# Another list of due dates, and other landing times, for a planner that writes a kernel's order

## The chip, the cores and the metric

The kernel runs on one core of a Trainium2 chip. A core has TensorE (PE), VectorE (DVE), ScalarE (ACT), GpSimd (POOL) and SyncE (SP), each with a queue of its own. The metric is the time of one execution on the device in microseconds.

## What is computed

Block-sparse attention is followed by a residual token-and-channel MLP, both for 4 batches of 768 tokens. Attention has 8 heads of 64; the MLP sees them as 512 channels, with 2048 hidden ones.

```python
mask = |block_i - block_j| <= 1, first and last block, 3 sampled blocks a row   # blocks of 32
attn = softmax(where(mask, q @ k.T / 8, -1e9)) @ v          # [4, 8, 768, 64]
x    = attn.transpose(0, 2, 1, 3).reshape(4, 768, 512)
u    = x + lam * einsum('ts,bsd->btd', w_tok, alpha1 * x + beta1)
out  = u + lam * (relu((alpha2 * u + beta2) @ w_ch1) @ w_ch2)
```

## The kernel before

**Tiling.** Two heads of one batch make a pair; there are 16 pairs (`NP`), four a batch. A pair's scores (two heads of 768 x 768, in 128-row tiles) are cut into 9 units of 1024 columns, so there are 144 units. For each unit PE makes QK into two PSUM banks (`sps`), ACT makes exp into an `eT` tile (L966, one of 7), and PE multiplies `eT` with `vext` (PV, L990) into a `gb` bank. In the first six pairs (`T0`) the mask rides in 24 additional rows of q and k (L928), and q and k come through PE transposes (L426), evacuated by DVE or ACT. In the later ten, three units are one batch (L947): two 64-row matmuls lie beside each other in the array, q and k come by transposing DMAs on SP's queue, and DVE multiplies the mask in (L971).

After a pair, DVE normalizes (L1006, L1009) into `x_sb` and makes `a1p` (L1162, L1173) with alpha1 and beta1 already multiplied by lam (`a1l`, `b1l`, L652 and L659); PE multiplies with the transposed w_tok (token matmuls, L1211); DVE adds them to `x_sb` (L1235) and makes `ub` (L1249), which is transposed into `uT`. After a batch's four pairs follow the channel products, in two halves of 384 tokens (`kk` from 0 to 7): 16 first products (`ch1`, L1358), each with a relu on DVE or ACT (L1405, L1397), and 3 x 4 groups of four second products (`ch2`, L1438), each 512 columns; the last group row of the last half is split into 384 and 128 columns. DVE adds the result to `x_sb` (L1460) and SP stores it (L1479).

**The order.** After a part written by hand (to L464), everything is an `Op` in a list `pl.ops` of 1408, with the engines that may run it, their prices in ns, a due date, and what it depends on. `Plan.run` (L170) plays time forward: whenever an engine is free, it starts that ready operation with the lowest due date for which buffers are there, and emits its instructions then. `pin_order` (L55) keeps each engine's order. So due dates and prices set only the order of each queue; on the chip semaphores decide the times. POOL issues all loads after the start (`load`, L539), SP the transposing DMAs and the stores.

Dates (`due0`) run from -46 to 208, one unit of date for each unit of attention. Then 67 seeds each move some dates near one place by random steps (L1493 to L1499):

```python
for op in pl.ops:
    if abs(op.due0 - mid) < wide and r.random() < part:
        op.due += r.gauss(0, step)
```

**What the planner takes for the first loads.** The load queue begins at `self.dma` = 6900; a load lands 700 ns after its share of the queue (L496 to L501). v of pair 0 lands at 7500 (L599), the second heads of the first q and k at 7000 and 6800 (`("f", i)`, L898), be2T at 6500 (L667). DVE is free from 6300, PE from 5950, ACT from 6100 (L469). On DVE wait at the start: three row copies (`row`, L905), two casts of the second heads (`fc`, L421), be2T's copy (`be2c`, L666) and the copies of v (`putv`, L1028). Matmuls on a constant (`fill`, L394) have dates from 1000: PE takes one only when nothing else is ready.

Of the kernel before, what the change touches and what calls it, by code (L numbers as in the profile page):

```python
# [44 lines left out]
EXPB = -0.35667494  # L45
T0 = 6
FINE = 3
SEEDS = [3340310007, 3340310011, 3340310015, 3340310024, 3340310026, 3340310027, 3340310065, 3340310070, 3340310081, 3340310120, 3340310138, 3340310152, 3340310166, 3340310177, 3340310178, 3340310179, 3340310340, 3340310371, 3340310405, 3340310518, 3340310537, 3340310574, 3340310590, 3340310686, 3340310729, 1340310788, 1340310806, 1340310822, 1340310954, 1340310957, 3340311162, 3340311192, 3340311406, 3340311549, 3340312202, 3340312526, 3340312534, 1340312821, 1340312995, 2340313211, 2340313318, 1340313338, 3340313793, 1340314038, 1340314057, 1340314590, 1340315664, 3340316245, 1363480032, 1363480039, 3363480372, 3363480518, 1363480765, 4363481891, 4363482185, 4363482912, 4363483188, 1382590026, 4382590413, 4382590423, 4382590431, 2382580781, 1382591202, 2382582015, 2382583582, 4382594112, 1382594473]
NFILL = 24
ORD = ((0, 2, 4, 1, 3, 5), (1, 3, 5, 0, 2, 4))  # L50
HF = 3 * S
# [51 lines left out]
class Plan:  # L103
# [3 lines left out]
    def __init__(self, pools, free):  # L107
        self.pools = {k: list(range(n)) for k, n in pools.items()}
        self.free = dict(free)
        self.ops = []  # L110
        self.users = {}
        self.slot = {}
        self.held = {}
        self.reader = {}
        self.shifted = False
        self.exps = 0
        self.dma = 6900.0
        self.ring = []
        self.occ = None
        self.loads = []  # L120
        self.hw = 0.0
        self.segs = []
# [47 lines left out]
    def run(self):  # L170
# [13 lines left out]
        while count:  # L184
            for r in [r for r in release if r[0] <= t]:
                release.remove(r)
                self.pools[r[1]].append(r[2])
            moved = True
            while moved:
                moved = False  # L190
                best = {}
                idle = [e for e in self.free if self.free[e] <= t]
                held = [(o.due, o.n) for o in cand if o.hold and o.ready <= t and len(self.pools["sps"]) == 2]
                held = min(held) if held else None
                for op in cand:
                    if op.ready > t:
                        continue
                    if held and op.need and (op.due, op.n) > held:
                        if any(n[1][0][0] in ("gb", "sps") for n in op.need):
                            continue  # L200
                    opts = [o for o in op.opts if o[0] in idle]
                    r = self.reader.get(op.reads)
                    if r and r[1] > t:
                        opts = [o for o in opts if o[0] == r[0]]
                    opts = [
                        o
                        for o in opts
                        if o[0] not in best
                        or (op.due, op.n) < (best[o[0]][0].due, best[o[0]][0].n)
                    ]  # L210
                    if not opts:
                        continue
                    taken = {}
                    for need in op.need:
                        p = self.place(need, taken)
                        if p is None:
                            break
                        taken[p] = taken.get(p, 0) + 1
                    else:
                        for o in opts:  # L220
                            best[o[0]] = (op, o)
                if not best:
                    break
                for op in cand:
                    if op.urgent and op.ready > t:
                        for o in op.opts:
                            if o[0] in best and best[o[0]][0].due > op.due:
                                if op.ready - t < best[o[0]][1][1]:
                                    del best[o[0]]
                if best:  # L230
                    op, (e, occ, vis) = min(best.values(), key=lambda x: (x[0].due, x[0].n))
                    for need in op.need:
                        p = self.place(need, {})
                        self.slot[need[0]] = (p, self.pools[p].pop(0))
                    op.start = t
                    op.eng = e
                    self.now, self.shifted = op, False
                    if callable(vis):
                        vis = vis(self, t)
                    if self.shifted:  # L240
                        for x in cand:
                            x.ready = max([d.vis for d in x.deps] + [0])
                    op.vis = t + vis
                    if op.reads:
                        self.reader[op.reads] = (e, op.vis)
                    self.free[e] = t + (self.occ or occ)
                    self.occ = None
                    for k in op.uses:
                        self.users[k] -= 1
                        self.held[k] = max(self.held.get(k, 0), op.vis)  # L250
                        if not self.users[k]:
                            release.append((self.held[k],) + self.slot[k])
                    if op.name[0] == "exp":
                        self.exps += 1
                    cand.remove(op)
                    count -= 1
                    for h in heirs.get(id(op), []):
                        h.left -= 1
                        if not h.left:
                            h.ready = max([d.vis for d in h.deps] + [0])  # L260
                            cand.append(h)
                    op.emit(op)
                    moved = True
            later = [x for x in self.free.values() if x > t]
            later += [r[0] for r in release if r[0] > t]
            later += [op.ready for op in cand if op.ready > t]
            if count and not later:
                raise RuntimeError(f"stuck: {[o.name for o in cand[:20]]}")
            if count:
                t = min(later)  # L270
# [3 lines left out]
def kernel(  # L274
# [54 lines left out]
    wtk = wk.tile([P, NT, S], BF, name="wtk", tag="w2b", bufs=1)  # L329
# [209 lines left out]
    def load(name, cost, due, emit, packet=70, **kw):  # L539
        return pl.add(name, [("POOL", 720, queued(cost, packet))], due, emit, **kw)  # L540
# [8 lines left out]
    def load_pair(pi, what="qkv"):  # L549
        b, n = divmod(pi, NPAIR)  # L550
        for w in what:
            key = (w, pi)
            src = dict(q=q, k=k, v=v)[w]

            def emit(op, key=key, src=src, w=w):
                nc.gpsimd.dma_start(ld[w][sl(key)][:], pair_ap(src, b, n))  # L556

            LD[key] = load(
                ("load",) + key,
                1020,  # L560
                9 * pi - (6 if w == "v" else 12 if pi < T0 else 20),
                emit,
                need=[(key, [(w, 0)])],
            )
# [6 lines left out]
    def bc_load(nm, t, src, due):  # L571
        def emit(op):
            nc.gpsimd.dma_start(t[:], src.unsqueeze(0).to_broadcast([P, DM]))

        BC[nm] = load(("bc", nm), 1640 if nm == "lam" else 640, due, emit)

    def emit_wtk(g):
        return lambda op: nc.gpsimd.dma_start(
# [17 lines left out]

        return f

    LD[("v", 0)] = landed(("v", 0), 7500)  # L599
    pl.slot[("v", 0)] = ("v", 0)  # L600
    pl.pools["v"].remove(0)
    for g in range(3):
        WT.append(load(("wtk", g), 2500, (-4, 1, 2)[g], emit_wtk(g)))
    bc_load("lam", lam_bc, moe_lam, 8)
    bc_load("a1", a1_bc, moe_alpha1, 8.1)
    bc_load("b1", b1_bc, moe_beta1, 8.2)
# [285 lines left out]
    for i in range(2):  # L892
        op = pl.dve(
            ("fc", i),
            dve(384, 2),
            1 + 0.1 * i,
            lambda op, i=i: first_cast(1, i, nc.vector.tensor_copy),
            deps=[landed(("f", i), 7000 - 200 * i)],  # L898
        )
        FC1.append(op)  # L900
    ROWS = []
# [143 lines left out]
    i = 0  # L1045
# [444 lines left out]
                    uses=[okey],  # L1490
                )

    for seed in SEEDS:  # L1493
        r = random.Random(seed)
        part, step = r.choice([0.02, 0.1, 0.3, 1]), r.choice([0.3, 1, 3])
        mid, wide = r.uniform(0, 300), r.choice([4, 12, 40])
        for op in pl.ops:
            if abs(op.due0 - mid) < wide and r.random() < part:
                op.due += r.gauss(0, step)  # L1499
    pl.run()  # L1500
    pin_order(nc, tc)

# [29 lines left out]
```

## Time and profile before

| | us |
|---|---|
| median of three runs | 306.15 (305.70 to 306.36) |
| the profiled execution | 305.65 |
| its span, first to last instruction | 303.9 |
| first planned matmul starts | 5.84 |
| the final stretch of `ch2` matmuls starts | 290.45 |
| DVE's last addition starts | 301.05 |
| TensorE's granted clock | 1.000 |

The span is what the profile shows; the time has another 1.75 us around it. A timeline line gives the start, the length, the engine, the line of the kernel, the operation, the tiles it writes and reads, their shapes, how many instructions are merged, and in brackets the engine's idle time before it with what ended it. Ends of matmuls are modelled, starts are not. Of the 368 matmuls of 512 columns at L1438, 339 are in the trace; the records of the others are missing.

The first loads by the trace, issue and landing in us:

| load | issued | landed | load | issued | landed |
|---|---|---|---|---|---|
| q, second head | 2.44 | 7.30 | k1 | 5.02 | 12.55 |
| k, second head | 1.78 | 5.81 | wtk1 | 5.72 | 14.40 |
| be2T | 2.19 | 7.06 | wtk2 | 6.26 | 16.27 |
| v0 | 3.07 | 8.72 | v1 | 6.79 | 17.67 |
| wtk0 | 3.76 | 10.60 | k2 | 7.49 | 18.56 |
| q1 | 4.33 | 11.60 | beta1 | 9.01 | 19.24 |
| alpha1 | 11.88 | 21.25 | lam | 12.84 | 21.89 |

### The profile page before, as it was taken

The numbers are of one execution on the slowest core, as the hardware profiler recorded it, in microseconds if no ns is written. First come the engines' busy times: TensorE is split into PE (matmuls) and PEld (weight loads), VectorE is DVE, ScalarE is ACT, GpSimd is POOL, SyncE is SP. The second block draws the span as 40 slices with busy tenths as digits, with TensorE's granted clock in tenths as the row PEclk, the third lists the DMA queues.
The fourth block names the chain that finished last, engine by engine and source line by source line (L and its number), as shares of the span: only waits on it lengthen the run. The fifth ranks groups of instructions, "written<-read, shape, count | busy, mean of one in ns | idle before, by whom it ended". The sixth has DMA issues, their size and how long they took to land.

```text
span 303.9 us, 7142 instructions
## 1 busy us (share of the span) xinstructions
PE 297.7 (98%) x2962; PEld 186.3 (61%) x2991; DVE 234.7 (77%) x443; ACT 175.8 (58%) x240; POOL 45.2 (15%) x71
## 2 busy tenths in 40 slices
PE   7999999999999999999999999999999999999997
PEld 3777878765665575556755665555665564555544
DVE  7679998999799699858977896878778763856532
ACT  4998799898587665778576454766567520000000
POOL 9467252413010102010000000000000000000000
PEclk9999999999999999999999999999999999999999
DMA  7999999999877717745262225024030005000011
GB/s 149 202 256 204 206 204 206 198 160 150 159 118 126 117 52 133 137 90 111 45 109 50 66 63 105 36 63 86 2 86 37 0 2 156 3 35 35 37 66 72
DMA packets 50672, 31.38 MB, mean 103 GB/s; under 512 B 27784, under 2 KB 47056, under 8 KB 50640
## 3 DMA queue, kind: packets, MB, share of 16 engines
q0 software_dynamic: 17520, 15.47, 33.7%
q1 hardware_dynamic: 32796, 15.06, 21.6%
q8 instruction: 23, 0.38, 0.5%
q10 hardware_dynamic: 324, 0.39, 0.4%
q14 instruction: 9, 0.07, 0.1%
HBM read 30.78 MB, written 6.29 MB: 122 GB/s over the span
## 4 chain that ended last, share of the span: by engine, by line
PE 88%; ACT 7%; DMA 2%; issue 1%; POOL 1%; DVE 0%; ACTq 0%; POOLq 0%
PE gb L1358 27%; PE gb L1438 27%; PE gb L1211 10%; PE gb L990 10%; ACT eT L966 7%; PE sps L947 4%; PE sps L928 4%; PE gb L947 3%; DMA v<-in_v_dram 2%; PE gb L426 1%; PE sps L1211 0%; POOL wtokT L378 0%; POOL be2T L386 0%; PE gb L394 0%; PE sps L1358 0%
## 5 line engine op out<-in xcount | busy, mean ns | idle before, releaser
L966 ACT ACTIVATE eT<-sps 128x1024 f16<-128x1024 f32 x114 | 110.9, 1033 | 6.8 <-PE sps L928 5.4
L1358 PE MATMUL gb<-uT,w1b 128*128 128x384 bf16 (+1 forms) x508 | 92.4, 326 | 0.0
L1438 PE MATMUL gb<-w2b,hts 128*128 128x512 bf16 (+2 forms) x371 | 88.4, 370 | 1.6 <-issue 0.2
L1358 PEld LDWEIGHTS <-w1b 128*128 128x128 bf16 x512 | 48.0, 98 | 32.7 <-issue 1.2
L971 DVE TENSOR_TENSOR eT<-eT,msk 128x1024 f16<-128x1024 f16 x90 | 58.8, 684 | 9.7 <-ACT eT L966 9.7
L1438 PEld LDWEIGHTS <-hts 128*128 128x128 bf16 x400 | 35.9, 97 | 36.9 <-issue 3.2
L990 PEld LDWEIGHTS <-eT 128*128 128x128 f16 x1152 | 47.9, 97 | 14.8 <-issue 3.8
L1405 DVE TENSOR_SCALAR hts<-gb,b1t 128x384 bf16<-128x384 f32 x72 | 44.3, 616 | 15.7 <-PE gb L1358 14.1
L966 ACT ACTIVATE eT<-gb 128x512 f16<-128x512 f32 x60 | 32.5, 594 | 40.2 <-PE gb L947 40.1
L990 PE MATMUL gb<-vext,eT 128*128 128x65 f16 x1152 | 53.2, 193 | 0.2 <-DVE vext L1028 0.2
L1397 ACT ACTIVATE hts<-gb,b1t 128x384 bf16<-128x384 f32 x55 | 31.8, 585 | 16.5 <-PE gb L1358 14.1
L1211 PE MATMUL gb<-a1p,wtokT 128*128 128x256 bf16 (+1 forms) x348 | 34.0, 250 | 0.0
L1211 PEld LDWEIGHTS <-wtokT 128*128 128x128 bf16 x360 | 29.2, 98 | 6.1 <-issue 1.6
L928 PE MATMUL sps<-qk 88*128 88x512 bf16 (+1 forms) x144 | 31.6, 325 | 0.4
L1460 DVE TENSOR_TENSOR ot<-x_sb,gb 128x512 f32<-128x512 f32 (+2 forms) x25 | 16.6, 663 | 16.2 <-PE gb L1438 15.9
L1235 DVE TENSOR_TENSOR x_sb<-x_sb,gb 128x512 f32<-128x512 f32 (+1 forms) x25 | 15.8, 641 | 5.2 <-PE gb L1211 5.0
L1009 DVE TENSOR_TENSOR x_sb<-gb,rcp 128x384 f32<-128x384 f32 x32 | 17.8, 557 | 1.1
L947 PE MATMUL sps<-qk 64*128 64x256 bf16 x180 | 17.9, 305 | 0.0
L947 PEld LDWEIGHTS <-qk 64*128 64x128 bf16 x240 | 9.3, 94 | 12.5 <-issue 8.2
L1249 DVE TENSOR_TENSOR ub<-x_sb,a_bc 128x512 bf16<-128x512 f32 (+1 forms) x26 | 16.2, 645 | 0.4
L556 POOL DMA_DIRECT2D q<-in_q_dram x15 | 10.8, 720 | 36.4 <-DMA qk<-q 28.8
L1162 DVE TENSOR_TENSOR a1p<-x_sb,a_bc 128x768 bf16<-128x768 f32 (+1 forms) x17 | 15.4, 905 | 0.2
(74 smaller groups left out, 165.0 us busy)
## 6 DMA issues: line engine op xcount, KB each, us to landing
out_dram<-ot SPq DMA_DIRECT2D x23, 256.0 KB, 2.0
v<-in_v_dram POOLq DMA_DIRECT2D x16, 192.0 KB, 6.8
q<-in_q_dram POOLq DMA_DIRECT2D x15, 192.0 KB, 6.6
k<-in_k_dram POOLq DMA_DIRECT2D x15, 192.0 KB, 7.0
w1b<-in_moe_w_ch_dram POOLq DMA_DIRECT2D x4, 512.0 KB, 12.1
w2b<-in_moe_w_ch_dram POOLq DMA_DIRECT2D x4, 512.0 KB, 13.2
qk<-qk SPq DMA_DIRECT2D x20, 96.0 KB, 3.5
wtk<-in_moe_w_tok_dram POOLq DMA_DIRECT2D x3, 384.0 KB, 8.7
```

The costliest lines, as they stand in the source:

```text
L928: nc.tensor.matmul(spsT[sl(key[0])][:, o : o + w], kx2[i][0:KC, a, ts(jt, P)], qx2[i][0:KC, a, c : c + w], start=True, stop=True,)
L947: nc.tensor.matmul(half(key, r)[:, o : o + w], kd[i][rows, h, g, :], qx2[i][rows, h, c : c + w], start=True, stop=True,)
L966: nc.scalar.activation(out_, in_, AF.Exp, bias=EXPB, scale=SCALE)
L971: nc.vector.tensor_tensor(out=e, in0=e, in1=msk[:, :, x : x + 512], op=ALU.mult)
L990: nc.tensor.matmul(bk[:, t * VW : t * VW + D + 1], eTt[sl(("eT", i))][:, ts(col, P)], vx[:, a, jt, 0 : D + 1], start=(r == 0), stop=(r >= ...
L1009: nc.vector.tensor_tensor(out=x_sb[:, s0 : s0 + NT, h * D : (h + 1) * D], in0=o[:, :, 0:D], in1=rc[:].unsqueeze(2).broadcast_to([P, NT, D] ...
L1211: nc.tensor.matmul(bank(bk)[:, j * wp * P : (j + 1) * wp * P], wtokT[:, s, ts(m * g + j, P)], a1p[sl(ak)][:, s, 0:wp, :].rearrange("p w c ...
L1358: nc.tensor.matmul(bank(bk)[:, 0 : HS + w0], w1b[:, dk, ts(f, P)], rhs[dk], start=(dk == 0), stop=(dk == 3),)
L1397: nc.scalar.activation(htsT[hk][:, f, :], bank(bk)[:, w0 : HS + w0], AF.Relu, bias=b1t[:, f : f + 1], scale=1.0,)
L1405: nc.vector.tensor_scalar(out=htsT[hk][:, f, :], in0=bank(bk)[:, w0 : HS + w0], scalar1=b1t[:, f : f + 1], scalar2=0.0, op0=ALU.add, op1=A ...
L1438: nc.tensor.matmul(bank(ck)[:, cs], htsT[hk][:, nk, ts(mt, P)], w2h["t"][:, nk, cs], start=(nk == 0), stop=(nk == 15),)
L1460: nc.vector.tensor_tensor(out=ot[sl(okey)][:, cs], in0=x_sb[:, b % NXB * NT + t, cs], in1=bank(ck)[:, cs], op=ALU.add,)
```

## The change

The seeds and their loop go. A list of 1408 whole numbers, one for each operation in the order of the list, is added to the dates in hundredths of a unit. Their standard deviation is 73 units without the fills, whose entries are 0 (the seeds' steps: 2.3, at most 11.9). Where two engines could start the same operation at the same moment, DVE is taken first. Prices and landing times of loads are other ones. No instruction is added or taken away; only the order of each queue, the engine of an operation that DVE and ACT can both do, and the buffer that it gets may differ.

```diff
-SEEDS = [3340310007, ..., 1382594473]
+DUE = [
+    -3320, -4973, -4124, -2497, -3795, -94, -4291, 3313, 2359, 2331, -861, -5555, -5734, -3452, -4351, -4448,
...
+]
...
-        self.dma = 6900.0
+        self.dma = 7650.0
...
-                    op, (e, occ, vis) = min(best.values(), key=lambda x: (x[0].due, x[0].n))
+                    op, (e, occ, vis) = min(
+                        best.values(), key=lambda x: (x[0].due, x[0].n, x[1][0] != "DVE")
+                    )
...
             LD[key] = load(
                 ("load",) + key,
-                1020,
+                1000,
...
-        BC[nm] = load(("bc", nm), 1640 if nm == "lam" else 640, due, emit)
+        BC[nm] = load(("bc", nm), 640, due, emit)
...
-    LD[("v", 0)] = landed(("v", 0), 7500)
+    LD[("v", 0)] = landed(("v", 0), 8600)
...
-        WT.append(load(("wtk", g), 2500, (-4, 1, 2)[g], emit_wtk(g)))
+        WT.append(load(("wtk", g), 2250, (-4, 1, 2)[g], emit_wtk(g)))
...
-            deps=[landed(("f", i), 7000 - 200 * i)],
+            deps=[landed(("f", i), 7100)],
...
-    for seed in SEEDS:
-        r = random.Random(seed)
-        part, step = r.choice([0.02, 0.1, 0.3, 1]), r.choice([0.3, 1, 3])
-        mid, wide = r.uniform(0, 300), r.choice([4, 12, 40])
-        for op in pl.ops:
-            if abs(op.due0 - mid) < wide and r.random() < part:
-                op.due += r.gauss(0, step)
+    for op, x in zip(pl.ops, DUE):
+        op.due += x * 0.01
     pl.run()
```

Some dates, before (with the seeds' steps) and after (with the list):

| operation | before | after | operation | before | after |
|---|---|---|---|---|---|
| row 1, 2, 3 | 0.5, 5.4, 8.1 | -102.0, -57.0, 43.4 | wtk 0, 1, 2 | -4.0, 0.9, 2.3 | -37.2, -48.7, -39.2 |
| casts of k, q | 2.1, 2.7 | -61.8, -50.0 | q1, k1, v1 | -3.8, -3.1, 3.3 | -58.6, -60.3, -31.5 |
| be2c | 34.9 | 10.6 | q2, k2, v2 | 6.4, 5.1, 10.9 | -37.5, -38.5, -31.1 |
| QK of unit 2 | -0.2 | -84.3 | alpha1, alpha2 | 7.5, 11.2 | -29.9, -26.9 |
| transposes of the second heads | -0.5, 0.0 | -73.2, -106.2 | lam, beta1 | 8.4, 5.7 | -17.0, 7.3 |
| a1l, b1l | 6.3, 8.1 | -21.8, 121.2 | k3, q3 | 15.4, 15.8 | -3.1, 8.6 |
| `ch2` half 6, third row, second group | 183.5 | 499.9 | `ch2` half 5, first row, second group | 151.3 | 585.0 |

The highest date of any `ch2` of half 7 is 353.9 afterwards. The stores (`out`) have dates of 0 before their steps, and offsets of -52 on the mean. The offsets of SP's transposing DMAs have standard deviations of 48 to 83 (`dq`, `dk`, `utd`).

## The prediction

> **What bounds the kernel now.** I read the page first, for which engine fills the span; then busy time by stretches; then the timeline of the first 10 us, of the stretch around 30 us and of the end; then the waits.
>
> ```profile
> span 303.9 us, 7142 instructions
> ...
> PE 297.7 (98%) x2962; PEld 186.3 (61%) x2991; DVE 234.7 (77%) x443; ACT 175.8 (58%) x240; POOL 45.2 (15%) x71
> ...
> PE 88%; ACT 7%; DMA 2%; issue 1%; POOL 1%; DVE 0%; ACTq 0%; POOLq 0%
> ```
>
> TensorE is the bound, and the change removes not one matmul. So a gain can come only from moments in which TensorE stands still. A busy share of 98% doesn't show them, because the ends of matmuls are modelled. I therefore took the start of every matmul from the trace and subtracted the usual pace of its form (median from one start to the next: 216 ns at 512 columns, 162 at 384, 109 at 256, 56 at 128, 30 at 65). Where more is left and another engine's semaphore came just then, I call it a stall. From the first planned matmul (5.84 us) the stalls are 1.0 us at 8.05 and 0.3 at 9.15; then by tens of us 0.33, 1.02, 0.25, 0.74 and 0.12 (10 to 60). From 60 to 250 us they sum to 1.6, but all except 0.2 to 0.4 stand at an edge of a row-tiled batch (L947). After 250 us there is nothing until the last product at 301.0.
>
> ```profile
> 10.00:20.00 10.00, 10.00 (x158) 7.97 (x155) 7.27 (x16) 9.85 (x11) 4.98 (x8) 1.00 1.19 235
> 20.00:30.00 10.00, 9.82 (x156) 7.70 (x154) 8.78 (x17) 9.02 (x10) 7.57 (x12) 1.00 1.25 215
> 30.00:40.00 10.00, 9.98 (x163) 8.24 (x160) 9.61 (x22) 8.07 (x9) 3.73 (x5) 1.00 1.25 206
> ...
> 60.00:250.00 190.00, 188.46 (x1856) 115.33 (x1880) 154.58 (x279) 124.93 (x182) 12.68 (x18) 1.00 0.48 85
> ```
>
> Columns: stretch, PE, weight loads, DVE, ACT, POOL, clock, DMA share, GB/s. Up to 60 us ACT is nearly as full as PE (9.85 and 9.02 of 10); later only PE is full, and DVE (81%) and ACT (66%) follow it. So there is something to win in the first 60 us, and after that mostly something to lose.
>
> ```profile
> 6.53 0.75 DVE L905 COPY qk<-qk 24x768 bf16<-24x768 bf16 x2
> ...
> 6.70 0.52 PE L394 MATMUL gb<-const-bfloat16-1.0 128*128 128x128 bf16 x6
> ...
> 7.65 0.34 DVE L421 CAST relp<-q2f 128x384 bf16<-128x384 f32 x1
> ...
> 8.05 0.34 PE L426 MATMUL gb<-identb,relp 128*128 128x128 bf16 x3 [0.83 <-DVE relp L421]
> ...
> 8.22 0.60 PE L928 MATMUL sps<-qk 88*128 88x256 bf16 x3
> ...
> 8.86 6.03 ACT L966 ACTIVATE eT<-sps 128x1024 f16<-128x1024 f32 x6 [0.46 <-PE sps L928]
> ...
> 28.11 2.17 PE L1211 MATMUL gb<-a1p,wtokT 128*128 128x128 bf16 x36
> ...
> 31.06 1.02 ACT L966 ACTIVATE eT<-sps 128x1024 f16<-128x1024 f32 x1 [2.04 <-PE sps L928]
> ...
> 297.56 0.69 DVE L1460 TENSOR_TENSOR ot<-x_sb,gb 128x512 f32<-128x512 f32 x1 [2.76 <-PE gb L1438]
> ...
> 301.05 0.29 DVE L1460 TENSOR_TENSOR ot<-x_sb,gb 128x128 f32<-128x128 f32 x1 [0.34 <-PE gb L1438]
> ```
>
> At 8.05 PE waits for a cast while QK of unit 2 (8.22) stands behind it, and ACT loses 0.46. At 28.11 PE runs 36 token matmuls in one block while ACT starves 2.04: an order that another list of dates can mend.
>
> **What the Trainium skill says.** Perfetto Trace Analysis, Identifying the Most-Contended Engine: matmul busy time is a bad measure of headroom. The trace agrees: 98% busy here still holds the stalls above. TensorE: Matmul & The Clock Gate, "Wait — 56ns, not 53.3ns?": 128/2.4 + 2.5 = 55.8 ns a matmul; the trace has 56. Same page, The mechanism: matmuls start and end strictly in program order; so at 8.05 one late operand held back a ready QK. TensorEngine Tiling (Array Packing), Key Properties: changing the tiling mode drains TensorE; here some 95 ns at each edge of the 30 row-tiled batches, about 60 x 0.095 = 5.7 us, which the change leaves in place.
>
> **The change, part by part**, against the profiled execution (305.65 us: span 303.9 and 1.75 around it; the median, 306.15, is 0.5 above it).
>
> 1. **First loads.** The planner started DVE at 6300 ns, placed two row copies (285 each) to 6870 and then the casts, whose data it took to be there at 6800 and 7000. Now it takes 7100 for both, so at 6870 it places be2c (date 10.6; 100) and the third row copy (43.4; 285) first. The casts come at 7255 and 7540, and the transposes' input is planned for 7540 + 420 = 7960 instead of 7155 + 420 = 7575. QK of unit 2 may start at 5950 + 677 + 1086 = 7713, when the first exp frees its bank; it now goes ahead of the transposes instead of behind them. On the chip the first exp ends at about 7.44 (6.47 + 1.94/2). QK 2 (109 + 215 = 0.33 us) moves into the hole from 7.05 to 8.05. The casts come some 0.45 later (a row copy of 0.37 and be2c), the transposes (0.33) at about 8.5, and with QK 3 (0.33) still fit before the first PV at 9.15. Value -0.3; bounds -0.46 (ACT's whole wait) and +0.1.
>
> 2. **Load queue and 10 to 30 us.** By the new dates POOL issues k1, q1, wtk1, wtk2, k2, q2, wtk0, v1, v2, a1, a2, lam, k3, b1 (before: wtk0, q1, k1, wtk1, wtk2, v1, k2, b1, q2, a1, lam). At the trace's own pace from v0's landing (8.72; about 1.0 us a q, k or v, 1.87 a wtk, 0.65 a vector), v1 lands at 19.3 (was 17.67), lam at 22.2 (21.89), b1 at 23.9 (19.24). So DVE's products with lam and hence the token matmuls (first at 28.05; b1l ended at 25.36) can't come more than about 1.5 us earlier, though the price of lam (1640 to 640) lets the planner count on it sooner. The later v1 is a new wait: its copy into vext stands in DVE's queue, with the evacuations of transposes behind it, for which PE's QK of the next pair waits. q1 (10.7 for 11.6) and k1 (9.7 for 12.55) come earlier and give transposes as filler. Stalls and fill matmuls here: 0.33 + 1.02 + 4 x 0.056 = 1.57. Up to 1.0 of it I hold to be lack of work. Value -0.6; bounds -1.2 and +0.4 (v1 late).
>
> 3. **Order from 30 to 60 us.** Stalls 0.25 + 0.74 + 0.12 = 1.1, each 0.1 to 0.2 behind an exp. A better mix of token blocks and QK removes more than half. Value -0.7; bounds -1.0 and +0.5.
>
> 4. **Order from 60 to 250 us.** The offsets are large: the seeds had moved dates by a standard deviation of 2.3 units, the table by 73, on a scale of 208. Every queue is reordered, SP's too: its stores stay ahead (dates about 0, now -52), but its transposes move among themselves by a standard deviation of 48 to 83, each with a wait for its data at which those behind it stand. 0.2 to 0.4 can be won. A low date makes PE take an operation the moment it is ready, so a late operand costs at once: the QK waits of 20 to 50 us are 0.13 to 0.24 each. Cover is ACT's idle time (34%) and DVE's (19%). Value +0.1; bounds -0.3 and +4.
>
> 5. **End.** Today the last product is a 128-column piece: 0.29 us of DVE, then a 64 KB store whose packets end 1.21 after its issue. Dates of 499.9 for a piece of half 6 and 585.0 for one of half 5 stand above all of half 7 (at most 353.9): if neither finds an earlier hole, a 512-column piece is last, 0.69 - 0.29 = 0.40 more on DVE and 1.67 - 1.21 = 0.46 more for 256 KB. Value +0.3; bounds 0 and +0.86.
>
> 6. **Tie-break and load prices otherwise.** 1020 to 1000 and 2500 to 2250 stand nearer to the 0.95 and 1.87 us of the trace; DVE first at equal dates only. 0, hidden by POOL's idle 85%; +-0.1.
>
> Sum: -0.3 - 0.6 - 0.7 + 0.1 + 0.3 = -1.2. 305.65 - 1.2 = 304.45, and 0.5 for the median: 304.95, so **305.0**.
>
> **Rivals.** No change (306.3): the work in 10 to 30 us is simply lacking (part 2 gives 0.2), part 3 gives 0.3, and the end costs its full 0.86: -0.3 - 0.2 - 0.3 + 0.1 + 0.86 = +0.16 on 306.15. For it: lam and b1 don't land sooner. Against: the 2.04 us block at 28 is an order, not a lack. Slower (308.0): in 60 to 250 us PE's strict order meets operands made just in time, to which the dates of before, near the natural order, gave room. Each costs about 0.18; the gain of 1.2 is gone with 7 of them, and from (1.2 + 0.6)/0.18 = 10 on it is measurably slower. With 17, one in every second batch: -1.2 + 3.1 = +1.9. For it: the size of the offsets. Against: the planner's latencies fit so well that 1856 matmuls hold under 0.4 us of stalls outside the mode edges.
>
> **Numbers.** Forecast 0.54, no change 0.2, slower 0.26. What this kernel's measurement can tell from no change is about 0.2%, 0.6 us. The forecast's own range is 303.2 to 305.5 (parts 2 and 3 at their good ends, or the end at its bad one). The whole reaches to 307.6, which leaves out the upper half of the slower case and a little below.
>
> **Right or wrong.** Part 1: QK 2 before 8 us, and ACT without the 0.46 wait. Part 2: the token matmuls before 28. Part 3: ACT's waits for PE from 10 to 60 us (3.7 us now) shrink. Part 4: waits of PE appear after 60 us: then I am wrong. Part 5: width of the last addition. The first planned matmul stays near 5.84, the last product moves from 301.0 to about 299.5.

## The result, and the profile after

| | before | after |
|---|---|---|
| median, side by side | 306.29 us (305.70 to 306.36, 6 runs) | 305.83 us (305.59 to 306.14, 6 runs) |
| ratio, 95% interval | | 0.9989 [0.9976, 1.0002] |
| the profiled execution, its span | 305.65, 303.9 | 306.14, 304.4 |
| DVE's last addition starts | 301.05 | 300.68 |
| from there to the end of the span | 2.85 | 3.72 |

The forecast was 305.0, 1.2 us less than before. 0.46 us less was measured, and the interval includes no change. On two other chips the same kernel came out slower (below), so the 0.46 is not a firm gain. The two profiled executions differ the other way round, +0.49: that of before is among the fastest of its kernel, that of after the slowest of its six. Single profiles of this kernel scatter by half a microsecond; what follows rests on stretches, not on the difference of two spans.

The page of after, its busy time and its chain of work:

```profile
span 304.4 us, 7164 instructions
...
PE 300.4 (99%) x2991; PEld 187.9 (62%) x2991; DVE 233.5 (77%) x441; ACT 177.4 (58%) x242; POOL 44.6 (15%) x71
...
PE 96%; DVE 2%; ACT 1%; issue 0%; ACTq 0%
```

ACT has left the chain (7% before, 1% now) and PE fills 96% of it. The same stretches as before:

```profile
10.00:20.00 10.00, 9.94 (x151) 7.86 (x150) 7.59 (x17) 9.71 (x11) 4.18 (x8) 1.00 1.17 226
20.00:30.00 10.00, 9.87 (x159) 7.61 (x158) 8.78 (x18) 9.76 (x12) 7.44 (x11) 1.00 1.23 226
30.00:40.00 10.00, 10.00 (x165) 8.50 (x163) 8.30 (x18) 9.93 (x13) 3.78 (x6) 1.00 1.27 204
...
60.00:250.00 190.00, 190.00 (x1890) 115.82 (x1889) 155.59 (x283) 124.45 (x182) 14.10 (x20) 1.00 0.47 87
```

From 20 to 40 us ACT is busy 19.7 of 20 us (17.1 before): exp work is done earlier. PE's busy share again says little. So I measured PE's **lost time**: at each weight load, its start plus the matmul work still to come at the usual pace (fills are not work); what this sum grows by in a stretch is lost there.

| lost by PE, us | 5.8 to 10 | 10 to 30 | 30 to 60 | 60 to 250 |
|---|---|---|---|---|
| before | 1.68 | 1.64 | 1.38 | 7.07 |
| after | 2.20 | 1.59 | 0.42 | 7.17 |

(The values from 60 us on hold the edges of the row-tiled batches.) The start costs 0.52 more, 30 to 60 us gives 0.96, the rest is as it was: 0.39 won before the end, and the last addition indeed comes 0.37 earlier. The end gives back 0.87. The timeline of after:

```profile
7.57 0.95 PE L485 MATMUL gb<-const-bfloat16-1.0 128*128 128x128 bf16 x7
...
8.11 0.36 DVE L512 CAST relp<-k2f 128x384 bf16<-128x384 f32 x1
...
8.32 1.06 PE L1019 MATMUL sps<-qk 88*128 88x256 bf16 x3
...
9.17 0.74 PE L517 MATMUL gb<-identb,relp 128*128 128x128 bf16 x6
...
9.42 1.02 ACT L1057 ACTIVATE eT<-sps 128x1024 f16<-128x1024 f32 x1 [0.52 <-PE sps L1019]
...
26.92 0.33 PE L517 MATMUL gb<-identb,q 128*128 128x128 bf16 x3
...
29.57 1.17 PE L1302 MATMUL gb<-a1p,wtokT 128*128 128x128 bf16 x18
...
300.68 0.69 DVE L1551 TENSOR_TENSOR ot<-x_sb,gb 128x512 f32<-128x512 f32 x1 [2.30 <-PE gb L1529]
```

QK of unit 2 (8.32) now stands ahead of the second heads' transposes (9.17). But seven fills stand before it, and seven 128-column matmuls take 0.95 us, 107 ns from one start to the next where the usual pace is 56: the array still runs at half its clock, and does so until 9.7 us. ACT loses 0.52 at 9.42, where before it lost 0.46 at 8.86. Transposes of q of pair 3 come at 26.92, the token matmuls at 29.57 (28.11 before), now 18 in a block instead of 36. The last addition is 512 columns wide. The waits from 10 to 60 us have one line of note:

```profile
ACT eT L1057 <- PE sps L1019: 2.0, 5, 0.7
```

Before, ACT waited there 3.7 us, 2.0 of it at once; now 2.0 us, 0.7 at most.

### The profile page after: what moved, and what is told of

It reads as the page before. It is cut to its first block, busy times and chain, and to the rows that moved or that the text cites. A ratio compares the mean times of both kernels' runs of the same rounds, so it can differ in the third digit from the quotient of the medians.

```text
span 304.4 us, 7164 instructions
## 1 busy us (share of the span) xinstructions
PE 300.4 (99%) x2991; PEld 187.9 (62%) x2991; DVE 233.5 (77%) x441; ACT 177.4 (58%) x242; POOL 44.6 (15%) x71
## 4 chain that ended last, share of the span: by engine, by line
PE 96%; DVE 2%; ACT 1%; issue 0%; ACTq 0%
PE gb L1529 27%; PE gb L1449 27%; PE gb L1081 12%; PE gb L1302 10%; PE sps L1019 8%; PE sps L1038 4%; PE gb L1038 3%; PE gb L517 2%; PE gb L485 2%; DVE qk L578 1%; ACT eT L1057 0%; ACT qk L576 0%; DVE wtokT L578 0%; DVE ot L1551 0%; DVE x_sb L1100 0%
## 5 line engine op out<-in xcount | busy, mean ns | idle before, releaser
L1529 PE MATMUL gb<-w2b,hts 128*128 128x512 bf16 (+2 forms) x400 | 89.4, 370 | 0.0
L1062 DVE TENSOR_TENSOR eT<-eT,msk 128x1024 f16<-128x1024 f16 x90 | 59.6, 683 | 6.5 <-ACT eT L1057 6.4
L1529 PEld LDWEIGHTS <-hts 128*128 128x128 bf16 x400 | 36.7, 98 | 38.9 <-issue 1.9
L1081 PEld LDWEIGHTS <-eT 128*128 128x128 f16 x1152 | 44.3, 97 | 10.8 <-issue 2.2
L1081 PE MATMUL gb<-vext,eT 128*128 128x65 f16 x1152 | 47.9, 193 | 0.1
L1488 ACT ACTIVATE hts<-gb,b1t 128x384 bf16<-128x384 f32 x55 | 31.5, 581 | 21.4 <-PE gb L1449 19.1
L1302 PE MATMUL gb<-a1p,wtokT 128*128 128x256 bf16 (+1 forms) x360 | 37.0, 251 | 0.0
L1019 PE MATMUL sps<-qk 88*128 88x512 bf16 (+1 forms) x144 | 32.6, 336 | 0.2
L1326 DVE TENSOR_TENSOR x_sb<-x_sb,gb 128x512 f32<-128x512 f32 (+1 forms) x26 | 16.7, 641 | 2.9 <-PE gb L1302 2.6
L1097 DVE RECIPROCAL rcp<-gb 128x6 f32<-128x6 f32 x32 | 6.1, 192 | 13.3 <-PE gb L1081 13.2
L647 POOL DMA_DIRECT2D v<-in_v_dram x15 | 10.6, 703 | 36.6 <-DVE vext L1119 24.9
```

Source lines behind the costliest of these rows:

```text
L1019: nc.tensor.matmul(spsT[sl(key[0])][:, o : o + w], kx2[i][0:KC, a, ts(jt, P)], qx2[i][0:KC, a, c : c + w], start=True, stop=True,)
L1062: nc.vector.tensor_tensor(out=e, in0=e, in1=msk[:, :, x : x + 512], op=ALU.mult)
L1081: nc.tensor.matmul(bk[:, t * VW : t * VW + D + 1], eTt[sl(("eT", i))][:, ts(col, P)], vx[:, a, jt, 0 : D + 1], start=(r == 0), stop=(r >= ...
L1302: nc.tensor.matmul(bank(bk)[:, j * wp * P : (j + 1) * wp * P], wtokT[:, s, ts(m * g + j, P)], a1p[sl(ak)][:, s, 0:wp, :].rearrange("p w c ...
L1326: nc.vector.tensor_tensor(out=s, in0=s, in1=tp, op=ALU.add)
L1488: nc.scalar.activation(htsT[hk][:, f, :], bank(bk)[:, w0 : HS + w0], AF.Relu, bias=b1t[:, f : f + 1], scale=1.0,)
```

## The experiments

Theory at the start: the order of 30 to 60 us is as much better as forecast; the wide end takes most of it; dates and landing constants belong together. Rival: the new dates are no better, and what is won early is lost late. E1 to E4 share one chip (median of the kernel before there: 306.40), E5 to E8 a second (306.15), E9 to E11 a third (306.13).

**E1. The narrow end alone** (one number of the list, for `ch2` half 6, third row, second group).

```diff
-    ..., -9729, -9183, -20429, 31640,
+    ..., -9729, -9183, -20429, -18150,
```

> The changed kernel with one number of the list changed, so that the last pieces of half 6 come before half 7 and the 128-column piece is the last product again. Theory (the new order won about 1 us of TensorE's waits before 60 us, and the 512-column piece at the end gave 0.86 back: 0.40 on DVE, 0.46 in the store): 0.86 faster than the changed kernel's 305.83, so 305.0, ratio to the kernel before 0.996. Rival (the gain was lost in waits after 60 us, or by a cold TensorE clock at the start, and the end is hidden): 305.8, ratio 0.9985.

306.54 (305.84 to 310.0), ratio 1.002 [1.0, 1.004]. The edit does its part: the last addition is narrow again, and from it to the end of the span are 2.8 us instead of 3.72.

```profile
301.90 0.29 DVE L1551 TENSOR_TENSOR ot<-x_sb,gb 128x128 f32<-128x128 f32 x1 [0.34 <-PE gb L1529]
```

And yet the kernel is not faster: it comes there 1.2 us later than after did. Lost time from 10 to 30 us is 2.38 instead of 1.59, though nothing there differs in the code. PE waits for q of pair 3, which lands at 28.0 instead of 26.0:

```profile
28.07 0.34 PE L517 MATMUL gb<-identb,q 128*128 128x128 bf16 x3 [0.78 <-DMA q<-in_q_dram]
```

That was not expected, and became the question of E5 to E10.

**E2. The wide end in the kernel before.**

```diff
+    for op in pl.ops:
+        if op.name == ("ch2", 6, 2, 1):
+            op.due = 499.9
```

> The kernel before with one date changed (second group of the third row of half 6 at 499.9), so that it too ends on a 512-column piece. Theory: 0.86 slower than before, 307.15, ratio 1.0028. Rival (the end is hidden): 306.3, ratio 1.000.

307.23 (306.51 to 307.84), ratio 1.003 [1.0019, 1.004]: +0.83 us beside before.

```profile
302.06 0.69 DVE L1460 TENSOR_TENSOR ot<-x_sb,gb 128x512 f32<-128x512 f32 x1 [2.30 <-PE gb L1438]
```

From this line to the end of the span (305.8) are 3.74 us. The wide end costs its full bound of 0.86, in the old order too.

**E3. The new landing times and prices with the old dates**, and **E4. the list with the old ones** (the constants of the diff, exchanged).

> The kernel before with its seeds, but with the new prices and landing times of the loads. Theory A (better landing times are worth something by themselves at the start): 0.3 faster, 306.0. Theory B (dates belong to the constants under which they were found; the planner's own clock puts the last product 6.1 us later with them): slower, up to 312.

> The changed kernel with its list, but with the old prices and landing times. Theory A (the list makes the order, the landing times only the first 10 us): 305.5 to 306.5. Theory B (the list belongs to its constants; the planner's own clock is 30 us later with the old ones): 320 to 336.

313.02 (311.73 to 314.10), ratio 1.0209 [1.0181, 1.0237]; and 329.65 (328.88, 330.42), ratio 1.0766 [1.0741, 1.0792]. Neither half of the change is an improvement by itself. That is theory B of both: dates fit the constants that they come with; with others the planner's clock drifts from them, and the same dates order the queues badly. In E4 these stand out:

```profile
268.96 6.10 PE L1302 MATMUL gb<-a1p,wtokT 128*128 128x256 bf16 x36 [2.86 <-DVE a1p L1264]
280.68 9.58 PE L1449 MATMUL gb<-uT,w1b 128*128 128x384 bf16 x50 [5.29 <-DMA uT<-ub]
```

So large offsets can do what the slower rival feared, late operands on PE. With their own constants they do not: from 60 to 250 us PE waits for nothing in the trace of after.

**E5. The changed kernel again, on another chip.**

> The changed kernel as it is, once more beside the others, because the run with the 128-column piece last (306.5, up to 310.0) didn't show the 0.86 that its own end had won. Theory (the new order's loads land only just before TensorE needs them, so that executions with later landings lose 1 us and more between 20 and 30 us): it too spreads here, above 306.5 in some executions, median 306.5 to 307.5. Rival (something in the earlier order of half 6 costs): 305.8 as at first, with a spread of 0.6.

306.94 (306.23 to 309.5, 20 runs), ratio 1.0033 [1.0018, 1.0048]. Lost time is 2.90 from 10 to 30 us and 0.52 from 30 to 60: the better order is there, and 1.3 us are gone before it. The timeline:

```profile
26.28 0.41 PE L1081 MATMUL gb<-vext,eT 128*128 128x65 f16 x8
27.91 0.34 PE L517 MATMUL gb<-identb,q 128*128 128x128 bf16 x3 [1.22 <-DMA q<-in_q_dram]
```

PE has finished PV at 26.7, and q of pair 3 lands at 27.87. In the profile of after it landed at 25.97 and its first weight load took it at 26.89, with 0.92 to spare. In before it landed at 25.39 and was taken at 27.45, ahead of this line of before: 2.06 to spare.

```profile
27.67 0.33 PE L426 MATMUL gb<-identb,q 128*128 128x128 bf16 x3
```

The new order needs the load half a microsecond earlier and, even in its best trace, gets it half a microsecond later.

**E6. Narrow end, and q of pair 3 loaded earlier.** The order of the planner's operations is kept on all engines, except POOL's: this load goes ahead of beta1, alpha2 behind it.

```diff
+        q3, a2, b1 = at[("load", "q", 3)], at[("bc", "a2")], at[("bc", "b1")]
+        order.remove(q3)
+        order.insert(order.index(b1), q3)
+        order.remove(a2)
+        order.insert(order.index(b1) + 1, a2)
```

> The changed kernel with the 128-column piece last and, on POOL's queue alone, the load of q of pair 3 ahead of beta1 and alpha2 behind it; every other queue is the same instruction for instruction. q3 then lands some 1.2 us earlier. Theory (late landings): the stop of TensorE for pair 3's q (0.78 us in the traced execution) is gone, and the long times with it: 305.2 to 305.7. Rival (cold clock or something else spreads the times): as before this edit, 306.5.

304.97 (304.70 to 305.74), ratio 0.9964 [0.995, 0.9977]. The load lands at 25.4 and is taken at 26.9; 10 to 30 us lose 1.59.

**E7. Narrow end, and four matmuls on a constant** in PE's hole at 4.8 us, so that the full clock is granted sooner; and **E8. the same four in the kernel before.**

```diff
             cp(out=qkr[0][:, w, 0, o0:o1, r, :], in_=t[r * D : (r + 1) * D, o0:o1])
+        if w == 0:
+            keep_warm(4, P)
```

> The changed kernel with the 128-column piece last and four more 128-column matmuls on a constant in the gap that TensorE has at 4.8 us, where it waits for a cast. Theory (the clock is granted in full only after a long enough busy stretch, and in most executions only at 9 to 10 us, so that the planned order starts at half speed): full clock by 7 us, 0.5 to 0.8 faster than without. Rival (the gap isn't what delays the clock): same as without.

> The kernel before with the same four matmuls. Theory of the clock: 305.7 instead of 306.3, as in its traced execution, in which the full clock was granted at 4.5 us. Rival: 306.3.

305.99 (305.33 to 306.78), ratio 0.9993 [0.9985, 1.0]; and 305.91 (305.5 to 306.65), ratio 0.9995 [0.9988, 1.0001]. In both the full clock is first granted by 4.6 us, and lost time to 10 us is 1.73 and 1.74: the old and the new order are equal once the clock is equal. But in these two traces the four matmuls did not bring the clock: they start at 4.75 us (E7) and 4.50 us (E8), when the pace was already the full one. What they do in other executions is open: in the traces without them the clock came at 8.8 to 10.1 us in five of six executions of the new start, at 3.6 in the sixth (E10), and in the old start at 4.5 in one and 9.3 in the other (E2). From 10 to 30 us both lose about 2.3 us, part of it to loads again: PE waits 0.56 us for q of pair 3 in E7, and 0.51 us for a w_tok load in E8.

**E9, E10, E11. The late load alone, and all edits together, beside the changed kernel.** E10 is E6 with the wide end of the change; E11 is E6 with the four matmuls of E7.

> The changed kernel once more, so that the two others have it on their own chip. Theory (q of pair 3 lands with about 1 us to spare, and not always): between 305.8 and 306.9, with PE waiting up to 1.2 us for that load near 27 us where it lands after 26.5. Rival (the order of the first 60 us is simply no better): about 306.3 with no wait for that load.

> The changed kernel with its 512-column end kept; only q of pair 3 is loaded earlier, ahead of beta1, and alpha2 later, behind beta1. Theory (the late load): 304.97 of the version with both edits, plus the 0.86 of the wide end, 305.8; closely spread (within 1 us), no wait for that load; faster than the changed kernel on the same chip by 0.3 to 1.1. Rival (what the two edits gave together came from the end alone): same as the changed kernel on the same chip within 0.2, and 0.9 of the 1.2 us gain stays with the end.

> All three edits: narrow end, earlier load of q of pair 3, and four matmuls on a constant in PE's hole at 4.8 us so that the full clock is granted near 4.5 instead of near 9.7 us. Theory (the three losses are separate and add up): lost time to 10 us falls by 0.5, so 304.97 - 0.5 = 304.5, and 1.6 us under the kernel before. Rival (what is done early in the first 10 us is waited for later, at the loads): 304.9 to 305.1, as without the four matmuls.

| | us | ratio to before |
|---|---|---|
| E9, the changed kernel | 307.13 (305.98 to 309.65) | 1.0036 [1.0018, 1.0054] |
| E10, q of pair 3 earlier, alpha2 later | 305.96 (305.54 to 306.47) | 0.9994 [0.9986, 1.0002] |
| E11, also narrow end and four matmuls | 304.77 (304.66 to 305.44) | 0.9961 [0.995, 0.9973] |

The new places of two loads, q of pair 3 and alpha2, are worth 1.17 us on this chip, and the spread shrinks from 3.7 to 0.9 us. The rival (the end alone made the gain of E6) is out. The timelines of POOL, first after, then E10:

```profile
16.17 0.56 POOL L664 DMA_DIRECT2D b_bc<-in_moe_beta_dram  x1 [0.24 <-DMA q<-in_q_dram]
18.66 0.71 POOL L647 DMA_DIRECT2D q<-in_q_dram  x1 [1.92 <-DMA wtk<-in_moe_w_tok_dram]
```

```profile
15.47 0.72 POOL L660 DMA_DIRECT2D q<-in_q_dram  x1 [0.27 <-DMA k<-in_k_dram]
17.10 0.56 POOL L677 DMA_DIRECT2D b_bc<-in_moe_beta_dram  x1 [0.91 <-DMA q<-in_q_dram]
```

It is issued 3.2 us earlier and lands at 24.77 instead of 25.97 to 29.0. Neither load was moved alone, so which of the two did it is not shown. The landings point to alpha2. From the landing of alpha1 to that of lam it is 1.0 to 1.4 us in E6, E10 and E11, where alpha2 comes behind them. Where alpha2 stands between them, it is 1.3 us in after, but 2.5 in E7 and 3.5 to 4.3 in E1, E5 and E9. An estimate from E5: q of pair 3 moved ahead of beta1 alone would have gained the 0.6 us between the landings of k of pair 3 and of beta1, and it was 1.2 us late.

E9 shows what a miss costs; it went beyond what was expected (at most 306.9, a wait of up to 1.2 us). PE's waits from 9 to 60 us, its timeline, the stretches around it, and the clock row and chain of its page:

```profile
PE gb L517 <- DMA q<-in_q_dram: 2.1, 1, 2.1
```

```profile
26.56 0.41 PE L1081 MATMUL gb<-vext,eT 128*128 128x65 f16 x8
29.05 0.34 PE L517 MATMUL gb<-identb,q 128*128 128x128 bf16 x3 [2.07 <-DMA q<-in_q_dram]
...
30.81 1.06 PE L1019 MATMUL sps<-qk 88*128 88x512 bf16 x2
```

```profile
27.00:30.00 3.00, 0.95 (x14) 0.81 (x15) 1.85 (x5) 0.91 (x1) 1.73 (x3) 0.99 1.26 198
30.00:34.00 4.00, 4.00 (x41) 3.03 (x39) 3.86 (x6) 2.79 (x3) 2.20 (x4) 0.58 1.29 201
34.00:40.00 6.00, 6.00 (x90) 5.08 (x88) 3.85 (x9) 5.73 (x8) 3.14 (x5) 1.00 1.26 206
```

```profile
PEclk9999899999999999999999999999999999999999
...
PE 88%; DMA 7%; POOL 2%; ACT 1%; issue 1%; DVE 0%; POOLq 0%; ACTq 0%
```

PE stands 2.07 us, and then the granted clock is 0.58 of full from 30 to 34 us: by the clock's record it is cut to half at 29.93 and back at 33.35. Lost time from 10 to 60 us is 5.52 (2.01 in after), 1.4 of the difference behind 30 us, where PE waits for no load any more. This execution took 309.65. The other long ones are of this kind. A cut of 3.4 us to half makes the mean clock of an execution 0.994. Seven of the 44 executions of E1, E5 and E9 have 0.994 or less, and these seven took 307.9 to 310.0 us; of the 25 of E6, E10 and E11 none has.

E11's last addition is narrow again and starts half a microsecond before that of after:

```profile
300.17 0.29 DVE L1566 TENSOR_TENSOR ot<-x_sb,gb 128x128 f32<-128x128 f32 x1 [0.34 <-PE gb L1544]
```

E11 is the best version run, 1.36 us under before. Beside E6 (0.9961 and 0.9964) the four matmuls are not told apart from nothing, so whether the three losses add up in full, to the 304.5 of the expectation, is not settled. The narrow end is: E6 against E10, each beside before on its own chip, is 0.0030, 0.92 us.

## Why the prediction was wrong, step by step

The forecast was a clear gain; what came is a change that can hardly be measured, within the range, and nearest to the "no change" rival, which had the missing work of part 2 and the full cost of the end right. The mechanism of parts 3, 4 and 5 held; part 2 failed, and part 1 gave nothing. In size, the 0.6 us of part 2 that did not come and the 0.56 us by which part 5 was priced too low make the miss; the 0.3 of part 1 was made up by part 3.

| part | forecast | runs showed |
|---|---|---|
| 1 first loads | -0.3 | 0 at equal clock; +0.5 between the two profiles |
| 2 load queue, 10 to 30 us | -0.6 | 0 when q of pair 3 lands in time; +0.7, +1.3 and +2.1 (E1, E5, E9) when not |
| 3 order, 30 to 60 us | -0.7 | -1.0 |
| 4 order, 60 to 250 us | +0.1 | +0.1 |
| 5 end | +0.3 | +0.86 |

**Part 1.** The order on DVE and PE is the forecast one: be2c and the third row copy ahead of the casts, QK 2 ahead of the transposes. But ACT's wait stayed. In after it is for QK 2 itself, which starts at 8.32 and runs at half the clock. With the full clock early (E11) QK 2 starts at 7.62, before 8 as forecast, and ACT no longer waits for it; but QK 3 stands behind both heads' transposes (9.20), and ACT waits for that one:

```profile
7.62 0.59 PE L1034 MATMUL sps<-qk 88*128 88x256 bf16 x3 [0.27 <-ACT eT L1072]
...
9.20 0.60 PE L1034 MATMUL sps<-qk 88*128 88x512 bf16 x3
...
9.84 1.02 ACT L1072 ACTIVATE eT<-sps 128x1024 f16<-128x1024 f32 x1 [0.44 <-PE sps L1034]
```

So the wait moves on by one unit and nothing is won. The clock decides the rest: 1.72 and 1.73 lost with it granted early (E11, E7), 1.68 and 1.74 in the old order (before, E8); 1.85 to 2.41 where it is late (after, E1, E5, E6, E9), 1.97 in the old order (E2). (E10 loses 2.07 by this count with an early clock, but its first planned matmul starts 0.3 us before the others'.) So the +0.52 between the profiles of before and after is mostly the luck of before's profile, not the change. The Trainium skill (TensorE: Matmul & The Clock Gate, What's actually happening) says that the clock rises after about 3.4 us of sustained work, in a window that runs freely, and so varies by 0.5 us. Here it varies by more: 3.6 or 9.5 us for the same instructions up to there (E10 and E9).

**Part 2** is the step that failed: it counted on -0.6, got nothing where all loads were in time, and named "v1 late" as its only new wait. v1 landed at 19.4, as forecast (19.3), and PE waited 0.2 us for its copy in after. The load that mattered is the next on the list after "k3, b1", where the list in the prediction stopped: q of pair 3, which PE's strict order needs at 26.9. A list of issues has to be followed to the last load that is used in the stretch, with a landing time and a time of need for each. From landings at some 1 us each behind b1 (23.9 by that pace), 24.9 would have been forecast, with two microseconds to spare; it took 26.0 to 29.0. So the mean pace alone wouldn't have given it: the spread of the landings counts, and that one trace doesn't show. "Up to 1.0 of it I hold to be lack of work" was right: with every load in time 20 to 30 us still loses 1.01 (E6, E10 and E11), and PE takes fills at 24.7 and 25.4 (E10, E11). What PE still loses in after is mostly waiting for exps: six gaps of 0.12 to 0.22 us between 13 and 30 us stand behind one, while ACT is busy 19.5 of the 20 us, so that it has hardly any room to come sooner. The token matmuls came later, at 29.57 and not before 28. Lam landed at 23.5 and beta1 at 25.0 (forecast 22.2 and 23.9), but DVE's product of beta1 with lam starts only at 26.94, 1.9 us after both are there: its order, which takes other work first, delays them too.

**Part 3** was right, a little too small: ACT's waits for PE fell from 3.7 to 2.0 us. The block of 36 token matmuls was an order and not a lack. All executions with the list and its own constants, except E9 with its cut clock, lose 0.3 to 0.8 from 30 to 60 us; those with the old dates and theirs 1.4 to 1.9.

**Part 4.** Right, and with it the slower rival is out: the view of PE's waits in after has no line from 60 to 300 us. The planner's latencies fit there; it was the loads, which it takes to be as punctual as everything else, that it misjudged.

**Part 5.** The mechanism was right and the size was off: "0.3" was a mean between a piece that finds an earlier hole and one that doesn't. The piece with 499.9 found no hole and came last. (The one with 585.0 must have found one: in E1, where its date is unchanged, the last product is the narrow one.) So the cost is the full 0.86: the runs gave 0.83 (E2), 0.92 (E10 against E6), and the two profiles 0.87.

**The sum** that the runs support: 0 - 1.0 + 0.1 + 0.86 = -0.04 with all loads in time, which is E10 (0.9994), and above it whatever a late load costs: E5 and E9, +0.8 and +1.0. The -0.46 of the first comparison lies 0.4 us below this sum; six runs on one chip, of which only the profiled one shows that the load landed in time, are not enough to say more.

## What to carry to other kernels

An order written from one trace is only as good as the slack of its loads: for each load in a tight stretch write down landing and need, and hold the slack against the scatter over several executions (here 26.0 to 29.0 us for one load), not against one trace. Look at the queue of loads before the matmuls: other places for two loads were worth as much (1.17 us) as the 1408 dates had won from 30 to 60 us (about 1.0). And look at the last instruction of such an order by hand: there a wide piece is paid in full, since nothing is left to hide it.

## What was not expected of the hardware

- **A stand of 2 us costs twice.** In E9 PE's wait of 2.07 us ended at 29.05, and at 29.93 the granted clock fell to half for 3.41 us. In E3 a wait of 1.99 us ended at 28.66, and a cut of the same length began at 30.14. Waits of 0.78 (E1), 1.22 (E5) and 1.30 us (E4, at 8.2) were not followed by one.
- **Gaps add up in windows of 3.41 us.** Eight traces record the clock's changes. In each, up to the end of the work, they lie whole multiples of 3.41 us apart (E9: full for 20.48 us, which is 6 of them, half for one, full again). I summed PE's idle time in each of these windows at full clock (what lies between two matmul starts beyond the usual pace, from 0.04 us on). The four windows with 1.94 (E3), 2.01, 3.41 (both E4) and 2.23 us (E9) were each followed by a cut; no window with 1.63 us or less was, and none lies between. One long wait is not needed: E4's cut at 266.28 comes after a window whose longest wait was 0.39 us, 0.2 us into the next wait. The Trainium skill (TensorE: Matmul & The Clock Gate, What's actually happening) speaks of an idle window of about 3.4 us. The length agrees with these traces; but the window need not be idle throughout.
- **Landings of the same queue scatter.** Lam was issued at 14.2 to 14.3 us in after, E1, E5 and E9; it landed at 23.5 in after and at 25.1 to 25.5 in the others. Q of pair 3, behind it, landed at 26.0 and at 27.9 to 29.0. Why the queue loses up to 3 us there, from alpha2 on, in some executions is open; it was not tried.
